# One fixed order of all steps from a table, with each two-operand step's engine, in place of a list planner

## The chip, the cores and the metric

One NeuronCore of a Trainium2 chip. It has five engines that run their own instruction streams and wait for each other by semaphores: TensorE (PE, matrix products; its weight loads are a row of their own, PEld), VectorE (DVE), ScalarE (ACT), GpSimd (POOL) and SyncE (SP, which issues the transfers). The metric is the device time of one execution in microseconds (us); a median of several runs is compared.

## The reference

Three layers in a row, in fp32. First a gated linear attention with a running stabiliser, over B=4 batches, H=8 heads, S=768 steps, D=40:

```python
for t in range(S):
    m_new = np.maximum(f_gate[:, :, t] + m, i_gate[:, :, t])
    f_stab = np.exp(f_gate[:, :, t] + m - m_new)
    i_stab = np.exp(i_gate[:, :, t] - m_new)
    m = m_new
    C = f_stab[..., None, None] * C + i_stab[..., None, None] * np.einsum('bhd,bhe->bhde', vt, kt)
    n = f_stab[..., None] * n + i_stab[..., None] * kt
    h_tilde = np.einsum('bhde,bhe->bhd', C, qt)
    denom = np.maximum(np.abs(np.einsum('bhd,bhd->bh', n, qt)[:, :, None]), 1.0)
    y[:, :, t] = o * h_tilde / denom          # o = sigmoid(o_gate)
x = y.transpose(0, 2, 1, 3).reshape(3072, 320)
h = np.maximum(np.maximum(x @ w1, x @ w2), x @ w3)      # 768 wide
x = h @ w_out                                           # FFN 1
h = x @ w_in                                            # 2048 wide
out = (h * np.clip(h + 3, 0, 6) / 6) @ w2_out           # FFN 2
```

## The kernel before

**Attention** runs in 24 groups g = (chunk of 128 steps, batch), four groups a chunk. A group's steps: transfers of q, k (`qs`) and of k, v, the output gate (`kvo`, in the first groups `kvg`); decays `fd` by two scans (line 575; in the first groups from a broadcast `bc` on PE, later from DRAM); `vt` and `vw`, v times gates (587, 594); score products `sc` and their product with the decays (609); `pv`, the weighted sum (673; in later groups with low parts `vr`, `pr`, lines 656 to 667, and short products, 679); `nm` (698), the denominator `rr` (705 to 707), `sg`, the sigmoid (622) times `rr` (711), `y` (716), its transpose `tr` (725) and x (731, and its low part 735, 736). For the state: `dc` (755), `ct` (765), `cn` (774) and its pieces `ch`, `cs` (782, 791), which the next chunk's `in` (636) reads. The gates of chunks 1 to 5 are computed in one go (360 to 431).

**FFN 1** runs over token blocks j of 2, 2, 4, 4, 4, 4, 4 groups (`BLK1`) and six column blocks k. For each (j, k): three products `h` (321), their running maximum `m` (862 on ACT, 864 on DVE), its high part `hh` (874 on ACT), its low part (878 on POOL), and the accumulation into `acc` (894, 896). Names carry the indices: h0_1_2 is block 0, column block 1, third matrix; w1_3_2 the weights of column block 3, piece 2. Weights arrive as 64-bit numbers and are taken apart: `a` (288) and `t` (297) on ACT, the join on DVE (301), the high part on ACT (829) and the low part `w` on POOL (308).

**FFN 2** runs over 48 quads n_ = 8j + p (six token blocks, eight pairs of column blocks). The products `T` and `Q` (1228) are a seven-product scheme for 2 x 2 blocks; `cc` (1275 to 1290) and `gg`, the high part on ACT (1302) and the low part (1306, two pieces of 512 columns a quad, all 96 pieces on DVE); `po` (1350) multiplies by the second weight.

**What sets the order.** Each step is entered with `P.add(engine, ns, priority, fn, r=..., w=...)`; steps are numbered as they are entered. `Plan.order` (167) is a list planner: it simulates the engines, takes the step that can start first (then by priority), shifts the priorities of 126 steps by a table `MOVED`, models TensorE's clock in `Clock`, and puts steps that have `lock` set on DVE or POOL, whichever ends first. The steps are then issued in the order of their planned start, so each engine's stream is fixed when the kernel is built. Where the plan leaves PE idle ahead of the first FFN product, the main loop at 1424 puts filler matmuls `wps<-junk` (1430), 41 of them. The same loop closes the pools gp1 and gp2, which hold the gates and the early `kvg` tiles, behind the last step that uses them, and opens xp and hp only then:

```python
if n == n_gates + 1:
    assert n_kvg < n_gates
    gp1.__exit__(None, None, None)
    late["right"] = [pool("xp", side="right"), pool("hp", side="right")]
```

`m`, `hh` and x2 tiles live in xp and hp, so the first FFN 1 result cannot be written before that.

Of the kernel before, what the change touches and what calls it, by code (L numbers as in the profile page):

```python
# [57 lines left out]
}  # L58
# [54 lines left out]
class Clock:  # L113
    WINDOW, WAKE, HOLD, SLOW = 3413.0, 0.69, 0.33, 1.9

    def __init__(c):
        c.end, c.full, c.busy = c.WINDOW, False, 0.0

    def pass_to(c, t):
        while t >= c.end:  # L120
            c.full = c.busy >= c.WINDOW * (c.HOLD if c.full else c.WAKE)
            c.end, c.busy = c.end + c.WINDOW, 0.0

    def run(c, t, ns, dense):
        c.pass_to(t)
        while ns > 1e-6:
            f = 1.0 if c.full else c.SLOW
            d = min(ns * f, c.end - t)
            c.busy += d * dense
            ns, t = ns - d / f, t + d  # L130
            c.pass_to(t)
        return t

class Plan:
    LAT = dict(PE=300, DVE=130, ACT=150, POOL=150)

    ALT = {  # L140
        128: dict(DVE=285, POOL=460), 256: dict(DVE=415, POOL=740), 320: dict(DVE=485, POOL=930), 512: dict(DVE=695, POOL=1290),
        -128: dict(DVE=285), -256: dict(DVE=415), -320: dict(DVE=485), -512: dict(DVE=695), -1: dict(POOL=1300),
    }
# [1357 lines left out]
```

## Time and profile before

| | us |
|---|---|
| median of 3 runs | 758.57 (755.49 to 759.45) |
| the profiled execution | 759.38 |
| its span in the trace | 757.6 |
| PE busy | 738.2 |
| DVE busy | 580.0 |
| ACT busy | 382.5 |
| POOL busy | 338.6 |

The span is cut further below into stretches. A row of stretches shows the start and end, the length, then for each engine the busy time and, in brackets, the count of instructions, then the mean clock granted to TensorE (1.00 is 2.4 GHz, 0.50 the lower level, 1.2 GHz), the busy share of the DMA engines and the rate. A row of the timeline shows the start, the length, engine, source line, operation, out<-in, shapes, and in square brackets the idle time ahead of it and what ended it. A row of groups shows count, busy time, the mean length of one in ns, and idle time ahead with its causes. Line numbers are those of the kernel before; in the kernel after most lines are moved by a few.

### The profile page before, as it was taken

What the parts mean: (1) busy time and instruction counts of PE and PEld (TensorE: products, weight loads), DVE (VectorE), ACT (ScalarE), POOL (GpSimd) and SP (SyncE); (2) the same over time, 40 slices, a digit from 0 to 9 for tenths busy, and PEclk for the clock granted to TensorE, in tenths of its full rate; (3) what the DMA queues carried; (4) which work ended last, traced back from release to release, by engine and by line L of the source; (5) the groups of instructions that cost most, each with busy time, mean ns of one, the idle gap of its engine ahead of it and who ended that gap; (6) DMA issues with size and microseconds to landing.
All of it is one profiled execution on the core that took longest, in us unless ns stands there. A gap on an engine that the chain in (4) does not pass through costs nothing.

```text
span 757.6 us, 15148 instructions
## 1 busy us (share of the span) xinstructions
PE 738.2 (97%) x5660; PEld 674.0 (89%) x5664; DVE 580.0 (77%) x1035; ACT 382.5 (50%) x847; POOL 338.6 (45%) x357
## 2 busy tenths in 40 slices
PE   8989998999999999999999999999999999999998
PEld 5779988887888788878888899999999999999998
DVE  5778887787876878899698898786687686776664
ACT  4566634441233223233667876655555655655543
POOL 3667998897987777677343132021021021011000
PEclk7659999999999999999999999999999999999999
DMA  8595465548578476652645620200300300200101
GB/s 270 168 285 183 145 214 176 164 171 213 195 232 267 134 214 190 199 192 92 189 126 176 212 84 19 91 1 2 91 1 1 91 1 1 91 2 1 35 2 36
DMA packets 47650, 93.90 MB, mean 124 GB/s; under 512 B 6872, under 2 KB 23864, under 8 KB 47096
## 3 DMA queue, kind: packets, MB, share of 16 engines
q1 hardware_dynamic: 47576, 92.92, 39.4%
q8 instruction: 45, 0.74, 0.4%
q14 instruction: 29, 0.24, 0.1%
HBM read 73.53 MB, written 17.65 MB: 120 GB/s over the span
## 4 chain that ended last, share of the span: by engine, by line
PE 78%; POOL 9%; DVE 6%; ACT 2%; issue 2%; DMA 1%; SPq 0%; POOLq 0%; DVEq 0%; ACTq 0%
PE po L1350 21%; PE h L321 20%; PE T L1228 11%; PE Q L1228 8%; PE acc L894 5%; PE sc L605 2%; PE acc L896 2%; PE pv L679 2%; PE in L636 2%; PE dc L755 1%; PE pv L673 1%; POOL q L511 1%; PE wps L1430 1%; POOL cs L791 1%; DMA raw<-in_qkf 1%
## 5 line engine op out<-in xcount | busy, mean ns | idle before, releaser
L321 PE MATMUL h<-x,w 128*128 128x512 f32 (+1 forms) x1008 | 222.4, 369 | 5.6 <-ACT m L862 5.1
L321 PEld LDWEIGHTS h<-x,w 128*128 128x128 f32 x1008 | 170.4, 192 | 33.9 <-ACT m L862 6.3
L1350 PE MATMUL po<-wo,gg 128*128 128x320 f32 x1152 | 192.3, 310 | 0.0
L1350 PEld LDWEIGHTS po<-wo,gg 128*128 128x128 f32 x1152 | 172.3, 189 | 0.0
L1302 ACT CAST gg<-cc 128x512 fp32r<-128x512 f32 x96 | 59.5, 621 | 60.5 <-DVE cc L1290 52.3
L1306 DVE TENSOR_TENSOR gg<-cc,gg 128x512 fp32r<-128x512 f32 x96 | 68.8, 718 | 27.4 <-ACT gg L1302 26.8
L1261 ACT COPY s<-T 128x256 f32<-128x256 f32 x144 | 53.4, 371 | 57.5 <-PE T L1228 35.2
L894 PE MATMUL acc<-hh,w 128*128 128x512 f32 (+1 forms) x252 | 75.0, 374 | 0.0
L878 POOL TENSOR_TENSOR hh<-m,hh 128x512 fp32r<-128x512 f32 (+1 forms) x42 | 54.8, 1305 | 39.5 <-ACT hh L874 36.0
L864 DVE TENSOR_TENSOR m<-h,m 128x512 f32<-128x512 f32 (+1 forms) x84 | 50.9, 606 | 23.8 <-PE h L321 15.8
L1286 ACT ACTIVATE cc<-cc,b 128x512 f32<-128x512 f32 x96 | 59.4, 618 | 7.4 <-DVE cc L1275 7.4
L1290 DVE SCALAR_TENSOR_TENSOR cc<-cc 128x512 f32<-128x512 f32 x96 | 55.1, 574 | 10.3 <-ACT cc L1286 10.0
L1275 DVE TENSOR_TENSOR cc<-Q,s 128x512 f32<-128x512 f32 x96 | 53.1, 553 | 11.8 <-ACT s L1261 8.6
L575 DVE TENSOR_TENSOR_SCAN fd<-fd,ident 128x512 f32<-128x512 f32 x40 | 60.5, 1517 | 1.1 <-DMA fd<-f_d 1.0
L874 ACT CAST hh<-m 128x512 fp32r<-128x512 f32 (+1 forms) x42 | 23.5, 558 | 64.7 <-PE acc L894 64.7
L1203 POOL TENSOR_TENSOR xa<-xr,xa 128x256 fp32r<-128x256 f32 x10 | 9.0, 902 | 103.0 <-ACT xa L1199 103.0
L1207 POOL TENSOR_TENSOR xs<-xr,xs 32x256 fp32r<-32x256 f32 x10 | 9.9, 994 | 99.4 <-ACT xs L1199 99.0
L894 PEld LDWEIGHTS acc<-hh,w 128*128 128x128 f32 x252 | 45.4, 191 | 7.1
L862 ACT COPY m<-h 128x512 f32<-128x512 f32 (+1 forms) x42 | 22.0, 525 | 47.7 <-POOL hh L878 31.2
L1284 DVE TENSOR_SCALAR cc<-T 128x256 f32<-128x256 f32 x48 | 20.2, 421 | 28.2 <-PE T L1228 28.2
L609 DVE TENSOR_TENSOR fd<-sc,fd 128x512 f32<-128x512 f32 x48 | 32.0, 681 | 12.5 <-POOL vw L594 11.0
L308 POOL TENSOR_TENSOR w<-t,w 128x384 fp32r<-128x384 f32 (+2 forms) x30 | 27.4, 926 | 21.7 <-ACT w L829 17.9
(307 smaller groups left out, 1525.0 us busy)
## 6 DMA issues: line engine op xcount, KB each, us to landing
kvo<-in_kvo SPq DMA_DIRECT2D x22, 488.0 KB
fd<-f_d SPq DMA_DIRECT2D x20, 512.0 KB
qs_d<-q SPq DMA_DIRECT2D x24, 320.0 KB
qs<-qs_d SPq DMA_DIRECT2D x48, 160.0 KB
raw<-in_w SPq DMA_DIRECT2D x18, 384.0 KB
rawo<-in_w2o SPq DMA_DIRECT2D x16, 320.0 KB
raw<-in_w2m SPq DMA_DIRECT2D x16, 256.0 KB
raw<-in_qkf SPq DMA_DIRECT2D x24, 160.0 KB
```

What stands on the lines that cost most here:

```text
L321: nc.tensor.matmul(ps, wt[:, a:a + 128], x[:, r], start=n == 0, stop=n == len(order) - 1)
L575: nc.vector.tensor_tensor_scan(out=half, data0=s.get(("bc", a), half), data1=ident4.rearrange("p h t -> p (h t)"), initial=0.0, op0=ALU.mu ...
L878: nc.gpsimd.tensor_tensor(out=t[:, 1], in0=T["m", j, k], in1=t[:, 0].bitcast(F32), op=ALU.subtract)
L894: nc.tensor.matmul(acc[a], wo[:, a * 128:128 + a * 128], h, start=first, stop=last)
L1228: nc.tensor.matmul(ps, w[0:rows, a], x[0:rows, b], start=start and n == 0, stop=n == 3, skip_group_check=not start)
L1261: nc.scalar.copy(s["s", two][:, i % 2], s["T"])
L1275: nc.vector.tensor_tensor(out=x, in0=y, in1=s["s", i == 0], op=ALU.add)
L1286: nc.scalar.activation(s["r"][:, a:b], src, AF.Relu, bias=b3)
L1290: nc.vector.scalar_tensor_tensor(out=s["cc"][:, a:b], in0=s["r"][:, a:b], scalar=6.0, in1=src, op0=ALU.min, op1=ALU.mult)
L1302: nc.scalar.copy(GG[j, p][:, 0, a:b], s["cc"][:, a:b])
L1306: eng.tensor_tensor(out=g[:, 1, a:b], in0=s["cc"][:, a:b], in1=g[:, 0, a:b].bitcast(F32), op=ALU.subtract)
L1350: nc.tensor.matmul(po[t], x, WO[2 * p + e][:, o:o + OC], start=first and z == 0, stop=last and z == 2)
```

## The change

The planner, the clock model and all durations and priorities go. A list `ORDER` holds the numbers of all 3276 steps in the order in which they are issued. Steps with two operands in SBUF are entered with `pick=True`; a set `POOLS` names those of them that run on POOL, the others run on DVE. Attention's vt, vw, ct, sg, y, vr, pr, cs, q and qs low parts are among them, the weights' low parts, hh's low part and gg's. `JUNK` gives the number of fillers ahead of five steps (27 in all). The result of FFN 1's first piece (j, k) = (0, 0) is held in attention's tiles `vr` and `pr` (named vrfirst and prfirst), and the pools are switched by a step `open_first`.

```diff
-class Clock:
...
-    def add(p, eng, ns, pr, fn, r=(), w=(), size=0, wait=0, dense=False, deps=(), rk=None, lock=0):
+    def add(p, eng, fn, r=(), w=(), deps=(), pick=False):
...
+        if pick:
+            eng = "POOL" if n in POOLS else "DVE"
...
     def order(p):
...
+        at = {n: i for i, n in enumerate(ORDER)}
...
+        return [p.ops[n] for n in ORDER]
...
+JUNK = {16: 9, 26: 4, 65: 3, 64: 1, 57: 10}
...
-            P.add("POOL", 1150, pr + 20, wlo, r=[C], w=[Wt])
+            P.add("POOL", wlo, r=[C], w=[Wt], pick=True)
...
+        def slots1(j, k):
+            return [("vr", "first"), ("pr", "first", 0), ("pr", "first", 1)] if (j, k) == (0, 0) else [("m", (j, k)), ("hh", (j, k), 0), ("hh", (j, k), 1)]
...
+                if w == 0 and (j, k) == (0, 0):
+                    T["m", j, k] = sb("vr", "first", [128, H, DP]).rearrange("p h d -> p (h d)")[:, 0:N]
+                    nc.scalar.copy(T["m", j, k], T["h", j, k, w])
...
-            P.add("POOL", 500 + 1.6 * N, -1000, hl, r=[M, ("hh", (j, k), 0)], w=[("hh", (j, k), 1)], lock=-1 if j > 4 else 0)
+            P.add("POOL", hl, r=[M, HH0], w=[HH1], pick=True)
...
+            def open_first():
+                gp2.__exit__(None, None, None)
+                gp1.__exit__(None, None, None)
+                late["right"] = [pool("xp", side="right"), pool("hp", side="right")]
+                late["xp"], late["hp"] = (x.__enter__() for x in late["right"])
...
+            ready = P.add("-", open_first, deps=users({"gm", "gf", "gi", "gmt", "fh", "sel", "own", "dls", "kvg"}) + [min(users({"ffn"}))])
+            for n in users({"m", "hh", "x2"}):
+                P.ops[n]["deps"].add(ready)
...
-                P.add("POOL", 0, WP2, lo, r=[CC(i) for i in z], w=[Gt(i) for i in z], rk=10**7 + 10 * n_, lock=256 * (b - a))
+                P.add("POOL", lo, r=[CC(i) for i in z], w=[Gt(i) for i in z], pick=True)
```

PE around the first FFN 1 product, before: group 2's transpose, group 3's `dc` and `pv`, group 4's `in` (six more of its products left out), the first three h products and group 3's transpose.

```order
L725 MATMUL tr2_627<-ident4_105,y2_596 128x128 x3
L755 MATMUL dc3_641<-vw3_613,kvo3_172 64x42 x8
L673 MATMUL pv3_659<-vt3_498,fd3_502 128x42 x8
L636 MATMUL in4_0_684<-cn0_281,qs4_494 128x42
L636 MATMUL in4_1_685<-cn0_281,qs4_494 128x42
...
L321 MATMUL h0_0_0_701<-x10_374,w1_0_0_676 128x256 x8
L321 MATMUL h0_0_1_720<-x10_374,w1_0_1_694 128x256 x8
L321 MATMUL h0_0_2_741<-x10_374,w1_0_2_414 128x256 x8
L725 MATMUL tr3_757<-ident4_105,y3_737 128x128 x3
```

And after, on PE again:

```order
L755 MATMUL dc1_322<-vw1_294,kvg1_218 64x42 x8
L673 MATMUL pv1_347<-vt1_269,fd1_238 128x42 x8
...
L725 MATMUL tr1_400<-ident4_105,y1_376 128x128 x3
L725 MATMUL tr0_412<-ident4_105,y0_338 128x128 x3
L325 MATMUL h0_0_0_419<-x10_404,w1_0_0_368 128x256 x8
L325 MATMUL h0_0_1_428<-x10_404,w1_0_1_296 128x256 x8
L561 MATMUL bc3_1_444<-fh_119,sel_118 128x128 x4
```

The first h product moved from behind the `pv` of group 3 to behind the transposes of groups 1 and 0, with ten fillers between `pv` and the transposes (left out); group 3's broadcast now stands behind it.

DVE in the stretch behind the first product, around group 4's state `cn4`, before:

```order
L643 TENSOR_TENSOR nm5_805<-in5_1_781,idt_108 128x168
L864 TENSOR_TENSOR m0_1_778<-h0_1_1_796,m0_1_778 128x256
L774 TENSOR_TENSOR cn4_837<-dc4_810,ct4_625 128x168
L301 SCALAR_TENSOR_TENSOR t1_3_3_835<-a1_3_3_819,t1_3_3_835 128x320
L609 TENSOR_TENSOR fd4_611<-sc4_0_823,fd4_611 128x512
```

The same engine and place after:

```order
L774 TENSOR_TENSOR cn4_923<-dc4_861,ct4_702 128x168
L711 TENSOR_TENSOR sg4_825<-sg4_825,rr4_919 128x320
L887 TENSOR_TENSOR hh0_2_848<-m0_2_725,hh0_2_848 128x256
L305 SCALAR_TENSOR_TENSOR t1_3_3_944<-a1_3_3_946,t1_3_3_944 128x320
L870 TENSOR_TENSOR m0_3_883<-h0_3_1_888,m0_3_883 128x256
L870 TENSOR_TENSOR m0_3_883<-h0_3_2_897,m0_3_883 128x256
L312 TENSOR_TENSOR w1_3_3_959<-t1_3_3_944,w1_3_3_959 128x64
L312 TENSOR_TENSOR w1_3_3_959<-t1_3_3_944,w1_3_3_959 128x256
```

sg, hh's low part and the weights' low part, POOL's before, stand in DVE's row; hh and m are column blocks 2 and 3 where m was column block 1.

FFN 2's quad 22 on DVE, before: its `cc` steps and both low parts of `gg`.

```order
L1275 TENSOR_TENSOR cc22_7543<-Q22_7477,s1_22_7482 128x512
L1290 SCALAR_TENSOR_TENSOR cc22_7543<-cc22_7543 128x512
L1284 TENSOR_SCALAR cc22_7543<-T22_7470 128x256
L1290 SCALAR_TENSOR_TENSOR cc22_7543<-cc22_7543,T22_7470 128x256
L1275 TENSOR_TENSOR cc22_7543<-Q22_7477,s0_22_7520 128x256
L1306 TENSOR_TENSOR gg22_7574<-cc22_7543,gg22_7574 128x512
L1290 SCALAR_TENSOR_TENSOR cc22_7543<-cc22_7543 128x256
L1306 TENSOR_TENSOR gg22_7574<-cc22_7543,gg22_7574 128x512
```

After, POOL's row around that quad (`xs` are sums and low parts of later token blocks' x):

```order
L1220 TENSOR_TENSOR xs13_7540<-xr3_7164,xs13_7540 32x256
L1318 TENSOR_TENSOR gg22_7553<-cc22_7531,gg22_7553 128x512
L1216 TENSOR_TENSOR xs33_7613<-xr3_7164,xs33_7613 128x256
L1318 TENSOR_TENSOR gg22_7553<-cc22_7531,gg22_7553 128x512
L1216 TENSOR_TENSOR xa223_7645<-xr3_7164,xa223_7645 128x256
```

Both low parts of this quad moved from DVE to POOL; of all quads 50 of 96 pieces did.

## Rows read from the trace of the kernel before

**Rows 1.** The page, busy time of each engine.

```profile
PE 738.2 (97%) x5660; PEld 674.0 (89%) x5664; DVE 580.0 (77%) x1035; ACT 382.5 (50%) x847; POOL 338.6 (45%) x357
```

**Rows 2.** Stretches: length, busy (count) of PE, PEld, DVE, ACT, POOL, clock.

```profile
0.00:54.20 54.20, 47.46 (x302) 35.87 (x306) 36.18 (x71) 30.99 (x71) 30.41 (x43) 0.69 0.77 234
54.20:132.00 77.80, 73.86 (x705) 70.43 (x704) 65.46 (x114) 40.26 (x92) 67.67 (x73) 0.94 0.56 188
132.00:406.60 274.60, 270.73 (x2103) 225.22 (x2102) 221.52 (x361) 104.25 (x232) 198.41 (x198) 1.00 0.60 185
406.60:747.20 340.60, 339.05 (x2510) 335.66 (x2509) 254.63 (x488) 203.59 (x445) 42.08 (x45) 1.00 0.15 45
747.20:757.60 10.40, 7.07 (x49) 6.80 (x47) 2.23 (x5) 3.40 (x7) 0.00 (x0) 1.00 0.19 64
```

**Rows 3.** The timeline of the opening: start, length, engine, line, step.

```profile
6.61 1.10 PE L560 MATMUL bc<-fh,sel 64*128 64x128 f32 x8
...
20.10 1.22 DVE L575 TENSOR_TENSOR_SCAN fd<-bc,ident 128x512 f32<-128x512 f32 x1 [2.64 <-PE bc L560]
...
23.32 1.87 DVE L368 TENSOR_TENSOR_SCAN gm<-gf,gm,gi 32x640 f32<-32x640 f32 x1
...
27.21 0.69 DVE L609 TENSOR_TENSOR fd<-sc,fd 128x512 f32<-128x512 f32 x1
...
31.16 0.81 DVE L377 TENSOR_TENSOR gi<-gi,gm 32x640 f32<-32x640 f32 x1
...
32.74 0.17 DVE L705 SCALAR_TENSOR_TENSOR rr<-nm 128x8 f32<-128x8 f32 x1 [0.31 <-ACT nm L696]
...
40.40 0.39 DVE L735 TENSOR_TENSOR x<-tr,x 128x256 fp32r<-128x256 f32 x1
...
40.80 0.29 DVE L736 TENSOR_TENSOR x<-tr,x 64x128 fp32r<-64x128 f32 x1
...
45.76 1.29 DVE L301 SCALAR_TENSOR_TENSOR t<-a,t 128x384 uint32<-128x384 uint32 x1 [1.47 <-ACT t L297]
...
48.55 0.56 DVE L301 SCALAR_TENSOR_TENSOR t<-a,t 128x384 uint32<-128x384 uint32 x1 [0.30 <-ACT t L297]
...
54.17 1.22 PE L321 MATMUL h<-x,w 128*128 128x256 f32 x4
```

**Rows 4.** The chain that ended last, in order of time: start, length, step.

```profile
132.24 5.83 PE h L321 x24
...
146.15 1.25 PE pv L679 x48
...
459.62 1.76 PE po L1350 x12
466.51 1.76 PE po L1350 x12
```

**Rows 5.** Groups of instructions, 0 to 54.2 us: the fillers.

```profile
L1430 PE MATMUL wps<-junk 128*128 128x512 bf16 x37 | 14.4, 521 | 1.8 <-DVE junk L1383 1.6 <-issue 0.2
```

**Rows 6.** Groups by form on DVE, 54.2 to 132 us.

```profile
L575 DVE TENSOR_TENSOR_SCAN fd<-fd,ident 128x512 f32<-128x512 f32 x13 | 19.8, 1526 | 0.1
...
L301 DVE SCALAR_TENSOR_TENSOR t<-a,t 128x384 uint32<-128x384 uint32 x8 | 7.8, 981 | 0.3 <-ACT t L297 0.3
...
L698 DVE TENSOR_TENSOR nm<-pv,nm 128x336 f32<-128x336 f32 x5 | 2.4, 489 | 0.9 <-PE pv L673 0.7 <-PE pv L679 0.2
L705 DVE SCALAR_TENSOR_TENSOR rr<-nm 128x8 f32<-128x8 f32 x5 | 2.2, 441 | 0.0
...
L662 DVE TENSOR_TENSOR pr<-fd 128x512 f32<-128x512 f32 x2 | 1.9, 947 | 0.0
```

**Rows 7.** Groups by form on POOL, 54.2 to 132 us: weights' low parts.

```profile
L308 POOL TENSOR_TENSOR w<-t,w 128x384 fp32r<-128x384 f32 x8 | 9.9, 1246 | 4.9 <-DMA raw<-in_w 3.7 <-ACT w L829 1.0
```

**Rows 8.** Stretches: block 3's first product to block 4's.

```profile
190.60:251.30 60.70, 59.97 (x484) 50.08 (x481) 47.63 (x74) 19.51 (x41) 51.18 (x51) 1.00 0.70 224
```

**Rows 9.** The page, costliest groups: FFN 2's low parts on DVE.

```profile
L1306 DVE TENSOR_TENSOR gg<-cc,gg 128x512 fp32r<-128x512 f32 x96 | 68.8, 718 | 27.4 <-ACT gg L1302 26.8
```

More of the change, by code (lines that the diff above doesn't have):

```diff
@@ L108, in rows_of @@
     return b * S + c * L
-class Clock:
[L114 to L132, printed above, removed]
-class Plan:
[L138 to L143, printed above, removed]
+class Plan:
     def __init__(p):
-        p.ops, p.wrote, p.read, p.users = [], {}, {}, {}
-    def add(p, eng, ns, pr, fn, r=(), w=(), size=0, wait=0, dense=False, deps=(), rk=None, lock=0):
+        p.ops, p.wrote, p.read = [], {}, {}
+    def add(p, eng, fn, r=(), w=(), deps=(), pick=False):
         n, deps = len(p.ops), set(deps)
@@ L165, in add @@
+        p.ops.append(dict(n=n, eng=eng, fn=fn, deps=deps, pick=pick, wrote=set(w), tags={t[0] for t in (*r, *w)}))
         return n
     def order(p):
[L168 to L175 removed]
@@ L250, in order @@
-        assert len(res) == len(p.ops), "a step never comes"
-        p.end = max(done.values())
-        return sorted(res, key=lambda o: (o["at"], o["n"]))
+        at = {n: i for i, n in enumerate(ORDER)}
+        assert len(at) == len(p.ops) and all(at[d] < at[o["n"]] for o in p.ops for d in o["deps"])
+        return [p.ops[n] for n in ORDER]
 def body(tc, ctx, qk0, qkf, kvo, ig, fg, w1, w2m, w2x, w2o, out):
@@ L1182, in x_prep @@
             after = [("q", j - 1, 1)] if j else [left]
-            P.add("SP", 3500, pr, ld, r=[("x2d", i) for i in src] + after, w=[R(i) for i in range(4)], size=2 * 4 * 128 * 1024, rk=rk)
+            P.add("SP", ld, r=[("x2d", i) for i in src] + after, w=[R(i) for i in range(4)])
             def add(o, x, y, op=ALU.subtract):
                 go = lambda eng: eng.tensor_tensor(out=m(o), in0=m(x), in1=m(y), op=op)
-                P.add("DVE", 0, pr, go, r=[R(x), R(y)], w=[R(o)], lock=512)
+                P.add("DVE", go, r=[R(x), R(y)], w=[R(o)], pick=True)
             count = []
@@ L1209, in put @@
                 s["tag", name] = slot
-                P.add("ACT", 620, pr + 10 + n, hi, r=[left, R(i)], w=[slot], rk=rr)
-                P.add("POOL", 0, pr + 10 + n, lo, r=[R(i)], w=[slot], rk=rr, lock=256)
-                P.add("DVE", 0, pr + 10 + n, lx, r=[R(i)], w=[slot], rk=rr, lock=256)
+                P.add("ACT", hi, r=[left, R(i)], w=[slot])
+                P.add("POOL", lo, r=[R(i)], w=[slot], pick=True)
+                P.add("DVE", lx, r=[R(i)], w=[slot], pick=True)
             add(4, 2, 3, ALU.add)
@@ L1240, in quad, with prod @@
             Gt = lambda i: ("gg", n_, i)
-            def prod(where, w, x, start, pr):
+            def prod(where, w, x, start):
                 def go():
@@ L1412, in body @@
                 weights(k, p)
-        for seq, (what, j, k) in enumerate(order1()):
+        for what, j, k in order1():
             if what == "in":
                 for w in range(3):
-                    f_in(j, k, w, 4 * seq + w)
+                    f_in(j, k, w)
             else:
-                f_out(j, k, 4 * seq)
+                f_out(j, k)
         second_stage()
         order = P.order()
-        n_gates = max(n for n, o in enumerate(order) if o["tags"] & {"gf", "gi", "gm", "fh", "own", "dls"})
-        n_kvg = max(n for n, o in enumerate(order) if "kvg" in o["tags"])
         wps = psh.tile([128, 512], F32, tag="acc2", name="wps")
-        t_pe, fill = 500.0, True
         with tc.manual_schedule():
-            for n, o in enumerate(order):
-                if o["eng"] == "PE" and fill:
-                    while n and t_pe + 600 < o["at"]:
-                        nc.tensor.matmul(wps, junk[:, 0:128], junk, start=True, stop=True)
-                        t_pe += 430
-                    t_pe = max(t_pe, o["end"])
-                if n == n_kvg + 1:
-                    gp2.__exit__(None, None, None)
-                if n == n_gates + 1:
-                    assert n_kvg < n_gates
-                    gp1.__exit__(None, None, None)
-                    late["right"] = [pool("xp", side="right"), pool("hp", side="right")]
-                    late["xp"], late["hp"] = (x.__enter__() for x in late["right"])
-                if o["tags"] & {"acc2", "ffn"}:
-                    fill = False
-                prio(10 * n)
-                o["fn"](*[dict(DVE=nc.vector, POOL=nc.gpsimd)[o["eng"]]] if o["lock"] else ())
+            for i, o in enumerate(order):
+                for _ in range(JUNK.get(o["n"], 0)):
+                    nc.tensor.matmul(wps, junk[:, 0:128], junk, start=True, stop=True)
+                prio(10 * i)
+                o["fn"](*[dict(DVE=nc.vector, POOL=nc.gpsimd)[o["eng"]]] if o["pick"] else ())
         late["gp_"].__exit__(None, None, None)
```

437 lines of the change are left out of this document (171 added, 266 removed), and 143 rows, old and new, of tables (MOVED, ORDER, POOLS).

## The prediction

> **What bounds the kernel now.** I read the page's busy line first: TensorE (PE) is busy 738.2 of 757.6 us, VectorE (DVE) 580.0, GpSimd (POOL) 338.6 [rows 1]. That share is an average, so I then cut the span into five stretches at products whose start the chain and the timeline show [rows 2]: the attention that runs alone until the first FFN 1 product at 54.17 [rows 3], the mixed stretch until block 2's first product at 132.24 [rows 4], the rest of FFN 1, FFN 2, and the tail. From 132 on PE is busy 270.7 of 274.6 and then 339.1 of 340.6 us at granted clock 1.00 [rows 2]: no order of the same matmuls can gain more than some 5 us there. What is lost lies ahead of 132.
>
> How much, the same rows tell if fillers and the clock are taken out. In the first stretch PE is busy 47.46 us, of which 14.4 are 37 filler matmuls on a tile of ones [rows 5], at a mean granted clock of 0.69 (partly the lower of the two levels, 1.2 GHz): (47.46 − 14.4) × 0.69 = 22.8 us of work at full clock, so 54.2 − 22.8 = 31 us lost. In the second, 73.86 × 0.94 = 69.4 of 77.8, 8 us lost [rows 2]. What the reader is to see: a busy row of 88% hides that over half of the first stretch does nothing useful. The Trainium skill says so too (Perfetto Trace Analysis, Identifying the Most-Contended Engine): matmul busy time is no measure of headroom, weight-load busy time is a better one. The trace agrees, with PEld at 35.87 of 54.20 us; by the busy row alone the most that this stretch could give would be 6.7 us.
>
> **The change part by part.**
>
> *The opening.* Before, the first result waits for a buffer pool that opens only when every gate step and the early k/v/o tiles are through; four groups' attention and part of a fifth run first. After, the first product stands behind groups 0 and 1 and bc2 alone, and its result goes into two of attention's own tiles. Useful PE work ahead of it: 22.8 / 4 = 5.7 per group, two groups and one broadcast of 1.10 [rows 3] make 12.5 us. What sets its time is DVE, which has 26 us to do by then: 5.9 before the first scan's input, 5 scans of 1.22, 4 score products of 0.69, 4 joins of 0.56, the gate steps 1.87 + 3 × 0.81, x's low part 2 × 0.68, two w low parts, one vw and one y at about 0.5 each, two denominators of three steps of 0.17 to 0.2 [rows 3]. If DVE never waits the product comes at 26; at the share of the first stretch (36.18 of 54.20 us busy [rows 2]) at 26/0.67 = 39. I take the middle, 33, so DVE idles 7 us. PE then has lost 33 − 12.5 = 20.5 instead of 31: 10 us to be had, if nothing takes them back.
>
> *The stretch behind it.* PE needs 69.4 us and the 22.8 − 12.5 = 10.3 left over: 33 + 79.7 = 112.7 is the earliest for block 2's first product. But up to there the table takes 43 steps from POOL (115 to 72), nearly all of them to DVE: 10 w low parts of 384 columns, 2 of 320, 4 y, 5 vw, 4 vt, 2 sg, one vr, 4 cs, 5 hh, 2 q: 12,992 columns. The nearest row on DVE, 336 columns in 489 ns [rows 6], makes that 1.455 ns a column, 18.9 us. Group 8's nm and denominators, two pr and one qs move behind it (0.49 + about 1.0 + 2 × 0.95 [rows 6], and 0.95 for the qs by its like number of columns: 4.4). DVE: 36.18 + 65.46 + 18.9 − 4.4 = 116.1, and 7 idle in the opening: 123.1. So DVE and not PE sets this product, and two unknowns stand on it. One is idle time behind the opening: DVE was idle 12.3 of 77.8 us there [rows 2], 16%; on the 90 us in question between 0 and 14.3. The other is the price of running beside POOL: a scan takes 1526 ns on average where one alone took 1.22, a 384-column join 981 and once 1.29 us against 0.56, the first denominator step 441 against 170 ns [rows 3, 6]; 13 × 0.306 + 8 × 0.42 + 5 × 0.27 = 8.7 us of DVE's 65.5. With POOL at 72 steps instead of 115, between 0 and 8.7 of it goes. No row says which, so I take half of each: 123.1 + 7.1 − 4.4 = 125.8; ends 114.4 and 137.4. Group 8's pv, 48 products in 1.25 us where the chain shows such a group [rows 4], comes later on PE, 1.2 us. Gain: 132.0 − 125.8 − 1.2 = 5.0 us.
>
> *The rest of FFN 1.* There DVE gets more too. The tightest piece is block 3's first product to block 4's: DVE busy 47.63 of 60.70 [rows 8], and 13 us more by the same count of columns, 60.7 of 60.7. POOL goes from 48 to 35 steps, so the price of running beside it falls as well. Cover: the two h buffers, and the whole of the stretch, where DVE has 221.5 and some 25 more of 274.6 [rows 2]. I take 0; ends 0 and 6, about half of the idle 13 us that could turn into waits.
>
> *FFN 2.* The same 28 + 24 matmuls a quad; two po runs stand 6.89 us apart [rows 4]. 50 of 96 gg low parts go to POOL: DVE loses 50 × 0.718 = 36 us [rows 9]. On POOL a 384-column piece took 1246 ns [rows 7], so 512 columns 1.66 us, two in a quad 3.3 of 6.89, hidden since a quad's po stands two quads behind its gg. Without that cover each quad would lose 1.9; I take 0 and up to 1 at the last quad, one half of which is on POOL.
>
> *The fillers*, 41 issued before and 27 after, fill idle time only: 0.
>
> Sum: the profiled execution took 759.38, so 759.38 − 5.0 = 754.4; the median of the runs is 758.57, 0.8 lower, so 753.6.
>
> **The rivals.**
>
> *Contention goes (faster).* POOL is so much emptier that a DVE step seldom meets one. For it: the long steps above; the POOL steps removed are long ones, the w low parts of 1246 ns above all [rows 7]. Against: joins and scans still run beside the 72 that stay. Block 2's product then comes at the low end, 114.4 to 118; gain about 14, 744.6. The Trainium skill has a rule that bears on this (SBUF — State Buffer, Who interferes with whom): DVE's second port pair is GpSimd's own, an exclusive lock, so that a DVE instruction with both inputs in SBUF contends with a GpSimd one that reads SBUF. By it each w low part that moves to DVE is one contender less, and this rival gains; the stretched joins agree with it, but no row says how much of the stretch is left at 72 steps.
>
> *The opening doesn't open (no change).* The first product needs its weights' low part, which POOL does behind group 0's sg and three vt and which stands on join t1_0_0, the third on DVE; if the x tiles or this come at 39 or later, DVE's idle is 13 and the rest as taken: 123.1 + 6 + 2.7 + 1.2 ≈ 133, and nothing is gained: 757 to 760. For it: DVE's 33% idle in the first stretch, DMA already at 0.77 there [rows 2]. Against: x of groups 0 and 1 was complete at 41.1 even behind two more groups' steps [rows 3].
>
> *DVE becomes the bound (slower).* One mechanism, at two places: between the first product and block 2's, and from block 3 to block 4, DVE has everything to do and still waits for others as it did (16% and 13 of 60.7 us), while the price beside POOL stays. Block 2's product at 137.4, 5.4 + 1.2 late, and some 2 to 3 of the second place: 767. It decides once block 2's product comes after 131. For it: DVE's load to there grows from 101.6 to 116.1 while the time should shrink. Against: POOL's load falls by more than a third.
>
> **How the numbers follow.** Forecast (DVE gives back about half of the opening, block 2's product at 121 to 130): 0.46; contention goes: 0.12; the opening doesn't open, or DVE takes just all of it back: 0.18; slower: 0.24. The predicted time is 753.6. Its own range is 748 to 758, a third of it above 754.8, where a measurement can no longer tell it from 758.57 (0.5%, 3.8 us). So faster 0.31 + 0.12 = 0.43; same 0.15 + 0.18 = 0.33; slower 0.24. The range reaches to 742 (low end with the clock full) and 767 (the slower rival).
>
> **What would show it.** In the profile after: first h product near 33 (26 to 39) and fewer than 20 us of fillers and waits ahead of it; block 2's first product at 121 to 130; in the stretch ahead of that DVE busy over 90% and POOL down to some 60 us; scans under 1.45 us on average and joins under 0.85 if contention went down; the pitch of po unchanged at 6.89; the last h and first T some 5 us earlier and FFN 2 as long as before. Wrong if DVE has idle time in that stretch while PE waits for it (then the order, not the load, is the bound), if block 3 or 4 gains back or loses more than 3 us, or if FFN 2 differs by over 2.

## The result and the profile after

The changed kernel is slower: 766.45 us (763.13 to 767.78, 7 runs) against 758.61 (755.49 to 760.88, 7 runs), ratio 1.0091 with a 95% interval of 1.0065 to 1.0118. The profiled execution took 766.23, its span 764.5 us, 6.9 more than that of the kernel before. A ratio leaves out slow executions, those over 1.5% above the fastest of the same kernel (five of ten in e7 and two of ten in e14 below), while the medians are of all. The third of my rivals (slower, 767) named the right time, by luck: its mechanism was wrong.

The stretches of the kernel after, cut at the same products as [rows 2]; columns as there (start:end, length, then busy time of PE, PEld, DVE, ACT, POOL, granted clock, DMA share, GB/s):

```profile
0.00:33.56 33.56, 27.75 (x155) 18.92 (x155) 22.61 (x46) 13.32 (x30) 10.71 (x20) 0.74 0.62 197
33.56:142.37 108.81, 103.27 (x792) 97.35 (x793) 86.23 (x172) 58.41 (x135) 43.32 (x51) 0.75 0.56 177
142.37:415.44 273.07, 272.12 (x2154) 226.65 (x2153) 232.46 (x413) 102.24 (x226) 146.10 (x152) 1.00 0.62 190
415.44:754.10 338.66, 338.66 (x2509) 335.62 (x2508) 223.92 (x426) 201.24 (x452) 121.45 (x112) 1.00 0.15 46
754.10:764.50 10.40, 6.62 (x46) 6.36 (x44) 2.70 (x5) 2.96 (x7) 1.29 (x1) 0.96 0.19 65
```

Block 2's first product on the timeline, before and after (the chain in [rows 4] puts the one before at 132.24, the timeline at 132.04):

```profile
132.04 6.03 PE L321 MATMUL h<-x,w 128*128 128x512 f32 x24
142.37 0.86 PE L325 MATMUL h<-x,w 128*128 128x512 f32 x3
```

The first h product comes at 33.56 instead of 54.17, block 2's first product at 142.37 instead of 132.04: 20.6 us ahead, then 10.3 behind. From there to the last three h products, which stand in one row, the two kernels take 273.1 and 274.5 us, and from that row to the end 349.1 and 351.0. All of the loss lies between the first product and block 2's.

The reader is to see the column of the clock in the second row: 0.75, where the kernel before had 0.94. A finer cut of that row shows it at the lower level (0.50, 0.51) in three of the pieces:

```profile
33.56:43.60 10.04, 8.64 (x62) 7.67 (x62) 8.14 (x16) 7.91 (x17) 3.95 (x3) 0.84 0.53 147
43.60:58.30 14.70, 14.16 (x92) 12.92 (x92) 10.07 (x22) 8.17 (x23) 5.79 (x8) 0.50 0.77 238
58.30:74.00 15.70, 15.70 (x86) 14.81 (x85) 8.81 (x21) 8.64 (x19) 1.71 (x2) 0.50 0.46 146
74.00:84.00 10.00, 9.05 (x97) 8.26 (x96) 7.91 (x19) 5.15 (x13) 4.59 (x5) 0.99 0.87 290
84.00:100.80 16.80, 14.15 (x84) 13.27 (x82) 12.43 (x23) 6.13 (x15) 5.47 (x6) 0.51 0.48 147
100.80:142.37 41.57, 41.57 (x383) 40.42 (x383) 38.88 (x74) 22.41 (x51) 21.80 (x27) 0.95 0.49 160
```

From 58.3 to 74 us PE is busy in every us at 1.2 GHz, while DVE works 8.81 of 15.70 and POOL 1.71. In the kernel before three h products in a row stood at 54.17, the clock rose at 57.8 and stayed at 1.00 to 109:

```profile
57.80:109.00 51.20, 49.89 (x497) 46.92 (x498) 44.58 (x79) 29.14 (x71) 46.60 (x51) 1.00 0.51 168
```

In the kernel after the products of 256 columns come one or two at a time between attention's products of 42 and 128 columns. The clock rises at 74, behind two h products in a row, falls at 84 behind waits of 0.56 and 0.39 us, and rises again at about 101, again behind two in a row. The chain that ended last stays on PE from 43.67 to 74.2 us, but for 0.38 us on ACT; between 74.2 and 89.25 it runs mostly over DVE, ACT and POOL, and behind that over PE again. At the lower level 16 score products take 2.01 us of it, at the full clock 1.09:

```profile
43.67 3.64 PE pv L673 x16
...
58.37 2.01 PE h L325 x8
60.37 2.01 PE sc L606 x16
62.38 2.00 PE h L325 x8
64.39 2.01 PE sc L606 x16
66.40 3.57 PE pv L673 x16
...
89.25 2.24 PE h L325 x8
...
102.42 1.09 PE sc L606 x16
```

An account of the 10.3 us, from the first two rows of each kernel. Time lost to the lower clock (length times one less the clock): 33.56 × 0.26 + 108.81 × 0.25 = 35.9, before 54.2 × 0.31 + 77.8 × 0.06 = 21.5: 14.4 more. PE idle: 11.4 and 10.7, 0.7 more (idle time at the lower clock stands in both terms). Fillers at the clock of their stretch: 11.0 × 0.74 = 8.1 and 14.4 × 0.69 = 9.9, 1.8 less. Group 8's pv, moved behind, 1.2 less. That makes 12.1; 1.8 do not close. The account says where the time is, and not yet what would have happened at full clock: the experiments do.

### The profile page after: what moved, and what is told of

Its sections match the earlier page's. It is cut to its first block, busy times and chain, and to the rows that moved or that the text cites. A ratio compares the mean times of both kernels' runs of the same rounds, so it can differ in the third digit from the quotient of the medians.

```text
span 764.5 us, 15099 instructions
## 1 busy us (share of the span) xinstructions
PE 748.4 (98%) x5650; PEld 684.9 (90%) x5650; DVE 567.9 (74%) x1058; ACT 378.2 (49%) x847; POOL 322.9 (42%) x334
## 4 chain that ended last, share of the span: by engine, by line
PE 85%; DVE 7%; POOL 3%; DMA 2%; issue 1%; ACT 1%; ACTq 0%; SPq 0%; POOLq 0%; DVEq 0%
PE h L325 23%; PE po L1362 22%; PE T L1241 12%; PE Q L1241 9%; PE acc L902 6%; PE sc L606 3%; PE pv L679 2%; PE pv L673 2%; PE acc L904 2%; PE in L637 2%; PE dc L755 1%; DVE fd L576 1%; POOL pr L667 1%; PE tr L725 1%; DMA qraw<-in_qkf 1%
## 5 line engine op out<-in xcount | busy, mean ns | idle before, releaser
L325 PEld LDWEIGHTS h<-x,w 128*128 128x128 f32 x1008 | 176.7, 201 | 35.5 <-ACT w L829 2.8
L1318 POOL TENSOR_TENSOR gg<-cc,gg 128x512 fp32r<-128x512 f32 x50 | 65.7, 1319 | 151.0 <-ACT gg L1314 147.4
L1287 DVE TENSOR_TENSOR cc<-Q,s 128x512 f32<-128x512 f32 x96 | 53.2, 554 | 48.4 <-ACT s L1273 36.5
L1302 DVE SCALAR_TENSOR_TENSOR cc<-cc 128x512 f32<-128x512 f32 (+1 forms) x96 | 62.7, 654 | 35.5 <-ACT cc L1298 35.4
L1314 ACT CAST gg<-cc 128x512 fp32r<-128x512 f32 x96 | 58.9, 620 | 35.9 <-DVE cc L1302 32.6
L1298 ACT ACTIVATE cc<-cc,b 128x512 f32<-128x512 f32 (+1 forms) x96 | 58.9, 617 | 34.0 <-DVE cc L1287 33.6
L902 PE MATMUL acc<-hh,w 128*128 128x512 f32 (+1 forms) x246 | 73.2, 377 | 0.0
L576 DVE TENSOR_TENSOR_SCAN fd<-fd,ident 128x512 f32<-128x512 f32 x40 | 52.1, 1311 | 0.1
L667 POOL TENSOR_TENSOR pr<-pr 128x512 bf16<-128x512 f32 x21 | 29.9, 1430 | 33.4 <-DVE pr L663 33.2
L1318 DVE TENSOR_TENSOR gg<-cc,gg 128x512 fp32r<-128x512 f32 x46 | 33.7, 735 | 13.0 <-ACT gg L1314 12.7
L606 PEld LDWEIGHTS sc<-qs 40*128 40x128 f32 (+1 forms) x256 | 29.7, 223 | 4.0 <-issue 1.2
L606 PE MATMUL sc<-qs 40*128 40x128 f32 (+1 forms) x256 | 32.1, 314 | 0.2 <-DVE nm L644 0.2
L904 PE MATMUL acc<-hh,w 128*128 128x512 f32 (+1 forms) x82 | 30.0, 370 | 0.0
```

Of the source, the lines that this page charges most:

```text
L325: nc.tensor.matmul(ps, wt[:, a:a + 128], x[:, r], start=n == 0, stop=n == len(order) - 1)
L576: nc.vector.tensor_tensor_scan(out=half, data0=s.get(("bc", a), half), data1=ident4.rearrange("p h t -> p (h t)"), initial=0.0, op0=ALU.mu ...
L606: nc.tensor.matmul(s["ps", a][:, h], q[:, 1], q[:, 0], start=True, stop=True)
L902: nc.tensor.matmul(acc[a], wo[:, a * 128:128 + a * 128], h, start=first, stop=last)
L1287: nc.vector.tensor_tensor(out=x, in0=y, in1=s["s", i == 0], op=ALU.add)
L1298: nc.scalar.activation(s["r"][:, a:b], src, AF.Relu, bias=b3)
```

## The experiments

Two theories to begin with. C: TensorE's clock is the loss. D: the steps moved to VectorE are. All kernels are compared with the kernel before run beside them on the same chip.

**Fillers where the clock falls (e1).** Step 74 is group 2's pv.

```diff
-JUNK = {16: 9, 26: 4, 65: 3, 64: 1, 57: 10}
+JUNK = {16: 9, 26: 4, 65: 3, 64: 1, 57: 10, 74: 8}
```

> The changed kernel with 8 more filler matmuls right ahead of group 2's pv product, at the point (43.7 us) where TensorE's granted clock falls to the lower level in the changed kernel's trace; nothing else is changed. Theory C (the loss is TensorE's clock, at 1.2 GHz from 43.7 to 74 us and from 85 to 101 us while TensorE is busy): the fillers bring the clock back, block 2's first product comes at 133 to 138 us instead of 142.4, the time is 757 to 762. Theory D (VectorE's extra load sets that product): the fillers cost up to 3.4 us and give nothing, 766 to 770.

Measured: 767.3 (763.85 to 767.43, 4 runs), ratio 1.0106 (1.0070 to 1.0142). Block 2's product is at 143.35: neither of C's numbers, and the time is D's. Three of its stretches:

```profile
0.00:36.56 36.56, 31.61 (x155) 22.11 (x155) 22.75 (x46) 13.45 (x30) 10.92 (x20) 0.97 0.60 181
44.00:56.00 12.00, 11.04 (x93) 9.17 (x94) 10.22 (x21) 9.68 (x27) 3.95 (x6) 0.94 0.86 249
58.30:74.50 16.20, 16.20 (x97) 15.22 (x98) 9.46 (x23) 9.29 (x21) 2.28 (x3) 0.50 0.52 170
```

At 0.94 from 44 to 56 PE waits for others (the chain there runs over DVE: scans, denominator, vw, joins, y), and from 58 on it is at 0.50 as before. The 0.97 of the first row is not a clock that was granted. The trace's first record of the clock is at 30.7 us in this execution (at 5.9 in the kernel after), and what lies ahead of it is counted as full. The matmuls there have the length of the lower level: the first 16 score products, the kernel after first and this one second:

```profile
7.93 1.16 PE L606 MATMUL sc<-qs 40*128 40x128 f32 x16
9.55 2.08 PE L606 MATMUL sc<-qs 40*128 40x128 f32 x16
```

So this opening ran slower than that of the kernel after, and its first product came 3.0 us later (36.56), for which fillers that stand behind it are no cause. From the first product to block 2's it took 106.8 us against 108.8: the fillers gave some 2 us there, and this run's total does not settle between C and D. The openings of e2, e4 and e13 began in the same way, with first products at 36.04, 36.72 and 36.36. Behind 74 the chain that ended last, start and length, is a row of steps in series on DVE and POOL:

```profile
76.15 0.56 DVE t L305
...
77.38 1.38 DVE t L305
...
80.63 0.93 POOL y L716
...
85.67 2.74 DVE fd L576 x2
```

**The old placement in the new order (e2), and the new placement in the old order (e3).** e2 replaces the set POOLS by the engines of the kernel before; e3 replaces ORDER and JUNK and keeps POOLS.

```diff
-POOLS = {int(n) for n in """ ... the changed set ... """.split()}
+POOLS = {int(n) for n in """ ... the steps that ran on POOL before ... """.split()}
```

> The changed kernel's order and fillers with every two-operand step on the engine it had before the change. Theory D: VectorE is relieved, block 2's first product comes at 125 to 135 us, the time is 752 to 760. Theory C: TensorE still runs its first products at the lower clock, the time is 765 to 772 or more, since GpSimd's longer steps now stand in the changed order.

Measured: 814.6 (4 runs), ratio 1.0759 (1.0706 to 1.0812); block 2's product at 148.93, the row of the last three h products at 442.5. Theory D falls for the changed order: with VectorE relieved (76.01 us busy between the first product and block 2's, 86.23 after the change) that stretch takes 112.9 us instead of 108.8. C's 765 to 772 or more does not foresee 814.6 either: FFN 1's rest lost another 20 us. The changed order does not go with the old placement.

> The order and the 41 fillers of the kernel before, with the changed placement of two-operand steps and the first FFN 1 result in attention's tiles. Theory D: the placement alone makes it slower, 763 to 770. Theory C: the clock in the first 132 us is as before (0.69, then 0.94), and GpSimd's shorter list takes some contention away: 755 to 760.

Measured: 768.95 (765.65 to 770.66, 4 runs), ratio 1.0133 (1.0092 to 1.0175). By the total this looks like D, by the stretches it is not: block 2's product came at 130.85, 1.2 earlier than before the change, and the loss is behind it.

```profile
0.00:130.85 130.85, 116.63 (x1009) 100.70 (x1009) 113.11 (x224) 70.75 (x162) 58.17 (x71) 0.90 0.66 209
130.85:408.02 277.17, 272.47 (x2100) 225.90 (x2101) 238.01 (x411) 105.41 (x234) 145.24 (x152) 0.99 0.60 182
408.02:763.90 355.88, 347.35 (x2557) 342.53 (x2555) 240.43 (x426) 207.07 (x452) 123.29 (x111) 1.00 0.15 45
```

DVE is busy 113.11 of 130.85 us here, more than in either kernel, and PE is not late. But the clock of this execution was 0.90 to that product, and 0.83 in the kernel before; what the moved steps would cost the old opening at the same clock, this run does not show.

**Four h products in a row (e4).** The steps h (0,1,1) to (0,2,1), with what follows from them, are issued behind dc3 in ORDER instead of one by one between positions 192 and 234.

> The changed kernel with four h products (0,1,1) to (0,2,1) issued in a row, behind group 3's dc, instead of one at a time between narrow attention products; their followers move with them, no filler is added. Theory C: the clock rises behind that row (at about 64 us instead of 74), block 2's first product 3 to 6 us earlier, time 760 to 764. Theory D: no gain, 766 to 768.

Measured: 765.71 (762.02 to 767.0, 5 runs), ratio 1.0077 (1.0043 to 1.0112); block 2's product at 143.11, 106.4 us behind a late first product.

```profile
56.00:64.00 8.00, 5.93 (x38) 5.51 (x39) 3.65 (x7) 1.63 (x5) 3.01 (x3) 0.50 0.77 247
64.00:84.00 20.00, 17.28 (x164) 15.66 (x165) 16.70 (x39) 12.72 (x28) 6.61 (x7) 0.98 0.62 200
84.00:101.00 17.00, 14.34 (x92) 13.46 (x93) 12.43 (x23) 6.55 (x17) 5.48 (x6) 0.53 0.53 165
```

The row lifts the clock at 64 instead of 74, as expected, and PE then waits 2.7 of 20 us, with DVE at 16.70; from the first product to block 2's the gain is 2.4 us. I formed a third theory: from the first product to block 1's, the clock and DVE's series take turns, each a little ahead of the other, and lifting one in one place gives the time to the other.

**Fillers all along (e5), steps back to GpSimd (e6), both (e7).** e5 adds to JUNK, the later ones with ident's zeros and ones as operand, and puts short fillers into the h tile ahead of its products; e6 adds 13 steps to POOLS; e7 does both.

```diff
+JUNK = {16: 9, 26: 4, 65: 3, 64: 1, 57: 10, 74: 8, 104: 6, 92: 3, 136: 3, 96: 3, 101: 3, 143: 3, 151: 2}
...
+        HJ = {(0, 4, 0): 4, (0, 4, 1): 10, (0, 4, 2): 6}
...
+                for _ in range(HJ.get((j, k, w), 0)):
+                    nc.tensor.matmul(ps, late["jk"][:, 0:128], late["jk"][:, 0:N], start=True, stop=True)
                 products(ps, W1[k, w], 0, WC, T["x1", j][:, :, 0:N])
```

> The changed kernel with fillers all along the stretch from group 2's pv to the first product of block 1: 8 ahead of pv2, 6 ahead of dc3, 2 or 3 ahead of sc3, sc4, pv3, tr3, pv4 and dc4, and 4, 10 and 6 short ones into the h tile ahead of h (0,4,0) to (0,4,2). With 8 fillers alone the clock rose to 57 us and fell again to 74. Theory C (clock): held at 2.4 GHz the stretch from 59 to 101 us shortens by some 16 us less 5 for the fillers, block 2's first product at 130 to 137, time 756 to 761. Theory D2 (VectorE's row of waits from 74 to 98 us, steps in series, sets block 1's start whatever the clock): that start stays at 98 to 102, time 764 to 770.

Measured: 766.46 median, but 759.75 to 768.56 over 10 runs (ratio 1.0094, 1.0063 to 1.0126). The traced execution is the one of 759.75:

```profile
33.75:44.00 10.25, 9.18 (x64) 8.10 (x66) 8.34 (x17) 7.92 (x18) 3.95 (x3) 0.84 0.50 146
44.00:80.00 36.00, 33.77 (x317) 27.61 (x319) 29.22 (x62) 23.80 (x57) 15.22 (x17) 1.00 0.78 245
80.00:93.00 13.00, 10.41 (x66) 9.27 (x66) 9.39 (x20) 3.37 (x8) 3.69 (x5) 0.69 0.52 174
```

With the clock at 1.00 from 44 to 80 block 2's product comes at 136.69, 5.7 us earlier than after the change, and the span is 758.0, 6.5 shorter. Executions whose mean granted clock was 0.961 to 0.964 had spans of 764.7 to 766.8, two at 0.977 and 0.978 had 758.0 and 758.9; one at 0.982 had 764.7 and does not fit. It has no trace; a late first record of the clock, as in e1, raises such a mean.

> The changed kernel with 13 two-operand steps that stand on VectorE between 60 and 95 us (two hh low parts, two sg, five weights' low parts, two vw, one cs, one vt) put on GpSimd, which idles 50 us from 33 to 105; VectorE is relieved of 6 us there. Theory D2: block 1's first product at 94 to 97 instead of 99.4, block 2's at 137 to 140, time 761 to 764. Theory C: TensorE at the lower clock stays the bound, the time 765 to 768.

Measured: 766.83 (4 runs), ratio 1.0106 (1.0056 to 1.0156); block 2's product at 142.90, block 1's at 100.8. VectorE has 81.93 instead of 86.23 us to do up to block 2's product, and PE gains nothing: in this order the load on DVE alone is no cause.

> The fillers of the run before last and the 13 moved steps together. If clock and VectorE's series take turns as the bound, this is the only one of the three that gains much: block 2's first product at 126 to 133, time 750 to 757. Theory C alone expects what the fillers alone give, theory D2 alone what the moved steps alone give.

Measured: 767.04 median, 755.1 to 770.52 over 10 runs (ratio 1.0074, 1.0025 to 1.0124): inconclusive. One execution of 753.4 span at a clock of 0.986, the others of 763.5 to 768.8 at 0.967 to 0.984. The traced one (766.0) has block 2's product at 143.81.

> The kernel with fillers from pv2 on and 13 steps moved to GpSimd, once more: its executions lay between 753.4 us of span at a mean granted clock of 0.986 and 768.8 at 0.978, so one traced execution is not enough. If the clock and VectorE's series together set the stretch to block 1's first product, a traced execution with the clock at full there brings block 2's product to 127 to 134; if one that is mostly at full clock still has it at 140 or later, a third thing (a transfer, a weight) holds it, and the waits of TensorE name it.

The same kernel again: 768.19 (4 runs), ratio 1.0108 (1.0077 to 1.0138); block 2's product near 146 in the traced execution, where the clock was still at 0.50 from 36 to 50 and 56 to 64 us, and at the lower level through most of the opening, as in e1. The fillers of e7 do not hold the clock by themselves. PE's largest waits there are 2.0 us for y on POOL and 1.3 for x: no transfer holds it. What the clock gave back from the first product on, the fillers took: they stand for 13.0 us of PE's time there.

**The clock held throughout (e14).** The 13 steps on POOL, and 35 fillers more than e7, from the first broadcast on.

> The same 13 steps on GpSimd and fillers from the first step on: some 35 more ahead of the broadcasts, scores and pv of groups 0 to 2 and among the first h products, to hold the clock from 10 to 100 us. If the clock is the larger part of the loss, block 1's first product comes at 80 to 90 and block 2's at 124 to 132, time 748 to 757. If the series of waits is, fillers past the waits cost their own 3 to 8 us: 765 to 775.

Measured: 764.54 median, 756.48 to 774.93 over 10 runs, ratio 1.0023 (0.9984 to 1.0062). The traced execution has a span of 754.8 at a clock of 0.990; three others had 754.8 to 755.5 at 0.990 or 0.991. Its stretches, and the one of e13 from the first product to block 2's in the last line:

```profile
0.00:34.35 34.35, 26.84 (x177) 16.09 (x181) 23.61 (x48) 14.13 (x30) 11.39 (x20) 0.93 0.66 194
34.35:132.58 98.23, 95.00 (x850) 83.76 (x853) 81.01 (x155) 57.42 (x135) 53.56 (x65) 0.96 0.61 196
36.36:145.94 109.58, 104.45 (x840) 91.86 (x845) 81.53 (x157) 57.76 (x135) 53.68 (x66) 0.85 0.56 176
```

```profile
132.58 2.00 PE L325 MATMUL h<-x,w 128*128 128x512 f32 x8
```

Block 1's first product is at 90.58 instead of 99.43, block 2's at 132.58 instead of 142.37, 0.6 us past the upper ends that C had, and the span is 754.8. With the clock held and the 13 steps moved, the changed order reaches block 2 as early as the kernel before does at its own, lower clock, fillers included; e12 below, with the old opening and the clock nearly held, is there at 125.77. But five of the ten executions took 764 to 773 at clocks of 0.976 to 0.988 and one 760.9 at 0.993; they have no trace, and what held them stays open.

The traces in the changed order (e7 is as e13; e2, with the old placement, idles 11.8 us and is left out) close on one account of the stretch from the first product to block 2's: PE's own work, longer the lower the clock, then fillers, then idle time. Own work is PE busy less fillers; times the clock it is an estimate of that work at full clock.

| | stretch, us | clock | own work | at full clock | fillers | PE idle |
|---|---|---|---|---|---|---|
| after | 108.8 | 0.75 | 103.3 | 77.5 | 0 | 5.5 |
| e1 | 106.8 | 0.79 | 99.1 | 78.3 | 1.9 | 5.8 |
| e4 | 106.4 | 0.80 | 96.5 | 77.2 | 0 | 9.9 |
| e5 | 102.9 | 0.92 | 86.6 | 79.6 | 10.5 | 5.9 |
| e6 | 108.9 | 0.77 | 102.7 | 79.1 | 0 | 6.2 |
| e13 | 109.6 | 0.85 | 91.4 | 77.7 | 13.0 | 5.1 |
| e14 | 98.2 | 0.96 | 80.1 | 76.9 | 14.9 | 3.2 |

The own work at full clock is 77 to 80 us throughout, so the clock sets PE's time. In e14 it gives 23.2 us back, fillers take 14.9 of them, and PE idles 2.3 less: the 10.6 us of that stretch. Only e4 clearly shows idle time that grows where the clock rises, which the third theory expected everywhere. Each row is one execution.

**The early start undone (e10).** The first nine h products wait in ORDER until behind group 3's pv.

> The changed kernel with its first nine h products (0,0,0) to (0,2,2) held back until behind group 3's pv, in one row, as the kernel before has its first; nothing else is moved but what follows from them. If h products one at a time between attention's narrow ones are what keeps the clock low and attention late, attention's steps come earlier, the row of h runs at full clock, and block 2's first product comes at 132 to 140, the time at 756 to 764. If the early start is a gain that is only lost elsewhere, it comes later than 142.4 and the time is 767 to 775.

Measured: 776.77 (4 runs), ratio 1.0221 (1.0190 to 1.0251), block 2's product at 151.88.

```profile
34.00:65.00 31.00, 22.27 (x149) 19.77 (x148) 21.26 (x36) 17.32 (x42) 12.55 (x14) 0.50 0.73 217
65.00:109.00 44.00, 37.30 (x253) 35.49 (x253) 26.96 (x62) 17.73 (x41) 9.15 (x11) 0.69 0.43 131
```

Held back, they cost 9.5 us in this order: the early start is a gain, and C's forecast for this run fell. Without the h products PE's clock is at 0.50 all the more. With ten of them in a row at 65.08 it was at 1.00 from 70 to 80 us and fell again, behind a wait of 3.60 us for y:

```profile
80.65 0.87 PE L725 MATMUL tr<-ident,y 128*128 128x128 f32 x3 [3.60 <-DVE y L716]
```

So a row of h products does not keep the clock up where PE then waits.

**gg back on VectorE (e8).**

> The changed kernel with all 96 low parts of gg on VectorE as before the change. My term for FFN 2 (hidden, 0 to 1 us): 765 to 768, the time from the last h product to the end within 1 us of the changed kernel's 349. A rival, that the 50 pieces on GpSimd cost or gain something in each quad: FFN 2 differs by over 3 us.

Measured: 774.6 (4 runs), ratio 1.0218 (1.0159 to 1.0278). From the row of the last three h products to the end:

```profile
415.40:774.00 358.60, 349.22 (x2553) 342.11 (x2551) 248.33 (x480) 204.01 (x458) 58.09 (x63) 1.00 0.14 45
```

358.6 us, 9.5 more than the changed kernel's 349.1, and PE idles 9.4 of them, 3.9 at T waiting for ACT's copies and 1.5 at Q waiting for DVE. The rival was right: in this order the 50 pieces on POOL are not merely hidden, FFN 2 needs them there, though the kernel before had all 96 on DVE in 351.0.

**The order before, then the changed one (e9, e11).** The first 615 (e11: 1264) steps in the order and placement of the kernel before, with its 41 fillers, all others as changed. In short form (in the run's kernel the lists are written out; `BEFORE` stands for the old order):

```diff
-        return [p.ops[n] for n in ORDER]
+        return [p.ops[n] for n in BEFORE[:615] + [n for n in ORDER if n not in BEFORE[:615]]]
```

> The order, placement and 41 fillers of the kernel before for its first 615 steps (through block 2's first product), the changed order and placement for all steps behind. By the two traces the changed kernel loses 10.3 us up to that product and gains 3.4 behind it. If the loss lies in the opening and its clock alone, this gives block 2's product at 130 to 133 and a time of 752 to 756, under both kernels. If the changed order behind needs its own opening (buffers, weights loaded earlier), 757 to 762.

Measured: 756.59 (754.62 to 759.2, 12 runs), ratio 0.9970 (0.9946 to 0.9994), block 2's product at 131.90: under both kernels, by 0.3% against the kernel before. The loss lies ahead of block 2's product.

> The same for the first 1264 steps, through block 5's first product; behind it the changed order and placement. The traces put the changed kernel 11.9 us behind there and 6.9 at the end, 5 us gained. If that gain is the changed order's in the last part of FFN 1 and in FFN 2, the time is 752 to 755; if it is only the other side of an earlier loss, 757 to 760.

Measured: 759.4 (10 runs), ratio 0.9991 (0.9969 to 1.0014): no difference. In the traces e9 is 3.4 us behind the kernel before at block 5's first product (315.99 against 312.62) and 1.4 ahead at the end; e11, which changes the order only there, takes 445.8 us from there against 445.0. So the 5 us behind block 5 come only where the changed order also runs between blocks 2 and 5; it spends 3.5 us more there in e9 and 1.6 in the changed kernel.

**More fillers in that opening (e12, e15).** e12 adds 11 fillers ahead of dlp, sc3 and dc3, e15 12 more, most of them ahead of earlier steps. The edit from e9 to e15:

```diff
-JUNK = {16: 11, 42: 3, 43: 1, 38: 4, 30: 1, 87: 1, 60: 4, 52: 2, 70: 8, 74: 4, 117: 1, 92: 1}
+JUNK = {16: 11, 42: 5, 43: 2, 38: 6, 30: 3, 87: 1, 60: 5, 52: 3, 70: 8, 74: 5, 117: 2, 92: 5, 127: 3, 104: 5}
```

> The kernel made of the order before up to its step 615 and the changed order behind, with 11 more fillers ahead of the first FFN 1 product: 3 ahead of dlp, 4 more ahead of sc3, 4 ahead of dc3 (40 to 48 us, where the clock is at 1.2 GHz until 57.9 and TensorE waits about 2.8 us). If the clock is a bound there too (PE at the lower clock from 48 to 58, busy all the time), the first h product comes 1 to 3 us earlier or its row runs at full clock, block 2's first product at 128 to 131, the time 752 to 756. If VectorE's steps set that stretch, the fillers cost what they take beyond the waits, up to 2 us: 757 to 760.

Measured: 757.37 (751.09 to 761.39, 12 runs), ratio 0.9983 (0.9956 to 1.0010). The traced execution is the best of all, span 749.4:

```profile
40.00:48.40 8.40, 8.40 (x77) 6.06 (x75) 5.86 (x8) 5.89 (x14) 6.14 (x7) 0.81 0.98 301
48.40:104.00 55.60, 52.77 (x518) 49.36 (x516) 49.30 (x86) 32.03 (x76) 49.30 (x54) 1.00 0.56 187
```

The first h product comes at 48.4 instead of 54.1 and block 2's at 125.77. Its other executions had lower clocks; two at 0.964 took 759.6 and 759.7.

> The order before up to its step 615 and the changed order behind, with fillers enough (some 25 more than before) to hold the clock from 10 us to the first h product. One traced execution with 11 more fillers had its clock at full from 42 us on and took 749.4 of span; others of the same kernel fell to a clock of 0.964 and took 759.6. If more fillers hold the clock in every execution: 748 to 753. If the fillers themselves delay the opening: 756 to 762.

Measured: 756.05 (753.55 to 759.49, 8 runs), ratio 0.9958 (0.9933 to 0.9982). The clock is 0.977 to 0.988 in all of them; the spans are 751.8 to 757.8. The best version here, 0.4% under the kernel before, some 2.5 us of the 8 that e12's best trace promised. Its interval overlaps that of e9, so what the fillers add to e9 is not shown.

## Why the prediction was wrong

*The opening was right.* First product forecast at 33, measured at 33.56. The 33 was the middle of 26 and 39, and DVE had 22.61 us to do ahead of it instead of 26 and idled 11 instead of 7, so part of the agreement is luck. The early start was forecast to be worth 10 us; e10, which holds the products back in the changed order, loses 9.5, which is near but not the same quantity.

*"So DVE and not PE sets this product"* is the step that failed. I had PE's need at full clock (112.7) and DVE's sum (123.1), and took the larger. PE's work was sized right, 79.7 us against the 77.5 of the table; its clock was not, and at the 0.75 measured that work took 103.3 us of the 108.8. DVE's sum was sound: 22.61 + 86.23 = 108.8 us busy against 116.1 before any relief, and the relief is larger than the half that I took. Scans and joins in that stretch:

```profile
L576 DVE TENSOR_TENSOR_SCAN fd<-fd,ident 128x512 f32<-128x512 f32 x12 | 15.2, 1275 | 0.0
L305 DVE SCALAR_TENSOR_TENSOR t<-a,t 128x384 uint32<-128x384 uint32 x15 | 10.5, 708 | 2.0 <-ACT a L292 1.0 <-ACT t L301 0.9
```

1275 against 1526 ns and 708 against 981 [rows 6]. The rival by which contention goes was right in its premise and wrong in its result, since DVE was not what held. What was mis-sized is DVE's idle time: 7.1 taken for the stretch, with 0 and 14.3 as ends, and 22.6 measured (108.81 − 86.23); of DVE's waits in that stretch the trace puts 12.1 us down to PE, 7.6 to ACT and 1.6 to POOL. I took PE's floor at full clock, reading 0.94 in [rows 2] as a property of the stretch. It did not stay with the stretch once the order was another. The same rows said what the clock does with attention's products alone (0.69 in the opening, fillers and all), and the order listing showed that h products would now stand singly among just those. At 0.69 the 69.4 + 10.3 us of work would have taken 115.5 us, and block 2's product would have been put at 148.5; at the 0.75 that only the result shows, at 139.3.

*The slower rival* had the right time (767) by luck, from DVE's idle time and contention. The idle time was there, scans and joins were shorter, the first cause was missing, block 2's product came 5 us behind its 137.4, and its second place, block 3 to block 4, cost 0.7 us and not 2 to 3.

*Contention as a lock.* The rule of the Trainium skill that I weighed (SBUF — State Buffer, Who interferes with whom) holds in its direction: with POOL at 43.32 us busy in 108.81 instead of 67.67 in 77.80 [rows 2] scans and joins are shorter. It gave no time, since DVE was not the bound.

*The rest of FFN 1* was forecast at 0 (0 to 6): 273.07 against 274.5, 1.5 gained; block 3 to block 4 took 61.4 instead of 60.7 with DVE at 54.8 of it. *FFN 2*, forecast at 0 to 1: 349.1 against 351.0, and po still stands 6.89 us apart:

```profile
734.92 1.76 PE po L1362 x12
741.81 1.76 PE po L1362 x12
```

Right in the sum; but the reason, that the moved pieces are merely hidden, was only half of it (e8).

What is shown: the loss lies between the first product and block 2's; in the changed order neither the moved steps (e2, e6) nor the early start (e10) make it; PE at the lower clock holds the chain from 43.67 to 74.2 us, and the clock held there, with 13 steps off DVE, brings block 2's product back by 9.8 us (e14's traced execution; e5's, with fillers alone, by 5.7). What is not shown: that the changed opening is as good as the old one at the same clock, since e12 is 6.8 us ahead of e14 there with fewer fillers. What is only argued: that single h products among narrow ones are what lets the clock fall; e4 shows that a row of four lifts it, e10 that a row does not keep it up, and no run here spread the rows of the kernel before. Open is why executions of e5, e7 and e14 at like mean clocks differ by up to 18 us; that a mean counts the time ahead of the clock's first record as full is part of it in e13 (0.978 at 768.2), and may be in those without a trace.

## What to carry to other kernels

Where a reordering puts wide products singly among narrow ones, TensorE's floor is better taken at the clock that the narrow ones had; here that would have given 148.5 instead of 112.7, against 142.37 measured. Fillers that hold a clock cost PE time of their own: reckon own work over the clock, fillers and idle time apart before a theory is dropped because the total didn't move (e13). A mean clock is to be checked against the length of the same matmuls in another trace. A table of an order and a table of engines made together are not to be judged apart: the new order with the old placement took 814.6 us, and the old order with the new placement was no faster than the changed kernel (768.95).
